# Seven products in place of four corners in one more unit, and two levels in one more product

## The chip, the cores and the metric

The kernel runs on one core of a Trainium2 chip. The metric is the device time of one execution, in microseconds, taken as the median of several runs. A core has five engines with a queue each: TensorE (PE in the profile, its weight loads PEld), VectorE (DVE), ScalarE (ACT), GpSimd (POOL) and SyncE (SP). Transfers run on 16 DMA engines; SP and POOL issue them here. The engines meet through semaphores, and every queue is worked off in its own order.

## The reference

Everything is float32 at the core; the inputs arrive as 64-bit floats. A block of linear attention with decay feeds a two-layer network:

```python
# q, k, v: (4, 8, 768, 64); lam: (8,), w_in: (512, 2048), w_out: (2048, 512)
# attention, by blocks of 64 tokens, with a running state per head:
out[block] = (q k^T * decay mask) v + (q * decay) state
state      = lam^64 * state + (k * decay)^T v
x = out as (3072 tokens, 512)
h = x @ w_in
y = (h - tanh(h)) @ w_out
```

Most of the work is in the last two matrix products, 3072 x 512 x 2048 each.

## The kernel before

**Tiling.** The tokens are worked in six groups (g = 0 to 5) of 512: 128 positions of each of the four sequences. For a group, attention gives x (transposed, in two halves `xt0`, `xt1` of two sequences each), the up stage gives the hidden values, and the down stage gives the group's 512 x 512 outputs. The hidden width, 2048, is cut in four units (u = 0 to 3) of 512.

**Fewer products.** A 2 x 2 block product takes eight block products when done plainly. Strassen's scheme in Winograd's form takes seven, P1 to P7, at the price of sums: of the left factor (`S1` to `S4`), of the right factor (`T1` to `T4`) and of the products. `FACT` (L523) names the two factors of each. `up(g, u, n)` does product n of unit u (4 matmuls of 256 columns, L554) with what follows it: ScalarE copies and tanh, VectorE adds and subtractions. For unit 3 of the first group the four corners are done plainly, by `up_plain` (8 matmuls of 256 columns for each corner, L966), and so for unit 0. The sums of a unit's input weights are made by `sums_in(u)` in `ws[u]` and, for S3, in place in `w1[u]`; for unit 3 this runs in the second group (L1150).

**Two levels.** A product can itself be done in seven (a second level). In the down stage `down_twice(g, n)` does so with 28 matmuls of 128 columns (L907), where `down(g, n)` takes 16 of 256 columns (L850). `twice(g, n)` says which is used. The second level needs the quarters and sums of the right factor, which are the same for all groups and are made once, in DRAM (`fine`): `load_quarters(t)` reads four quarters of the factor of product `MADE[t]` (5, 6, 4, 7, 3), `quarters_alone(t)` writes three of them out as they are, and `factors_twice(t)` makes four differences on VectorE and writes each out. `TURNS` (L1118) spreads this over steps of the second group's up stage for t = 0 and 1. The quarters of t = 0 lie in four tiles of the ring, those of t = 1 in output tiles, those of later t in a hidden tile (`gS`) that is free then.

**The ring.** The down stage's weights stream from DRAM through eight tiles (`wb`), in the order of `stream`; GpSimd issues each load, when a tile is free (L793, L796, L799).

**From the third group on** the up stage has a second level too: `inner_steps(g + 1, n)` runs between the products P3 of the group before (`in_turn`). It needs sums of the tokens (`inner_tokens`) and of the weights (`inner_weights`).

**Order.** The program is written in the order that the loops give; a planner at build time orders each engine's queue by that order and by when operands come, except where `keep_in_program_order` (`tied`) holds it. The first group's up stage is a list by hand, `turns` (L1077): for each entry a product or corner, then so many blocks of the output weights to be rounded (`weights`; three ScalarE and two VectorE operations each), then pieces of the second group's attention. A pair of sequences has five or six pieces: transposes, scores (L359), states (L434, L438, L440), the output's part from the state (`att_inter`, L479), its part within the block (`att_intra`, L498), and for the second pair the sums T of the tokens (`att_sums`). While `held` is set, between the fourth and the fifth piece, the matmuls in between keep the order of the program.

**First down stage.** The first group's down products run over eight steps (kt); step kt needs a pair of weight blocks, rounded, and their sums (`sums_out`). Every third pair uses `ws[3]` and `ws[0]` as its tiles. `sums_first` and `sums_late` make the sums of the hidden values, unit by unit.

**Banks.** Products accumulate in PSUM. Products of a unit use the tags `ya` or `yb` (even or odd u), `w` and `z`, one bank each; attention and others use four banks `att`. A bank is taken again when what is in it has been read.

The functions that the diff touches, and what calls them:

Of the kernel before, what the change touches and what calls it, by code (L numbers as in the profile page):

```python
# [24 lines left out]
def kernel(  # L25
# [225 lines left out]
    def pair_tiles(kt):  # L251

        if kt % 3 == 2:
            return tuple(ws[u].rearrange("p x k c -> p (x k) c")[:, 0:4] for u in (3, 0))
        wt = wst.tile([128, 8, 256], F32, name="wt", tag="w")
        return wt[:, 0:4], wt[:, 4:8]

    def sums_in(u):
        a11, a12, a21, a22 = (w1[u][:, 2 * c:2 * c + 2, r] for r, c in ((0, 0), (0, 1), (1, 0), (1, 1)))
        s1, s2, s4 = (ws[u][:, x] for x in range(3))  # L260
        for dst, x, y, op in ((s1, a21, a22, AL.add), (s2, s1, a11, AL.subtract), (a21, a11, a21, AL.subtract),
                              (s4, a12, s2, AL.subtract)):
            tc.keep_in_program_order(nc.vector.tensor_tensor(dst, x, y, op=op))
# [461 lines left out]
    def twice(g, n):  # L725
        return n in TWICE and not (g == NG - 1 and n == 3) and not (g == 1 and n == 4) and not (
            g <= GI and n in (7, 3))
# [32 lines left out]
    def load_quarters(t):  # L760

        for i in range(2):
            for j in range(2):
                if t == 0:
                    x = late["pool"].tile([128, NU, 128], F32, name="wq", tag="wb", bufs=RING)
                elif t > 1:
                    x = hidden(GI + (t > 2), "S1")[:, 2 * i + j].rearrange("p m (v c) -> p (m v) c", v=2)
                else:
                    x = opool.tile([128, NU, 128], F32, name="oq", tag="o")
                tied(t > 1, nc.gpsimd.dma_start(out=x, in_=quarter_source(t, i, j)))  # L770
                quarters[t, i, j] = x
# [124 lines left out]
    def down_twice(g, n, zw):  # L896
# [30 lines left out]
        elif n == 7:  # L927
            nc.vector.tensor_tensor(res[g, 4], res[g, 4], o, op=AL.add)
            store(g, 21, res[g, 4], g < NG - 1)
            nc.vector.tensor_tensor(o, o, res[g, 5], op=AL.add)  # L930
            store(g, 22, o, g < NG - 1)
        elif n == 3:
            nc.vector.tensor_tensor(o, o, res[g, 5], op=AL.add)
            store(g, 12, o)
# [20 lines left out]
    def up_plain(u, cs):  # L955

        hm = {}
        for c in cs:
            a, t = divmod(c - 11, 10)
            tag = ("yb", "w")[a ^ t] if u == NU - 1 else ("ya", "yb", "z", "w")[2 * t + a]  # L960
# [105 lines left out]
    for u, n in ((1, 2), (1, 6), (1, 5), (1, 7), (2, 1), (1, 4), (1, 3)):  # L1066
        up(0, u, n)
        weights(ready["done"] + 1 + (n == 2))
        if n == 5:
# [7 lines left out]
    turns = [(2, 5, 0, ()), (2, 2, 0, ()), (2, 6, 0, p0[0:1]), (3, 11, 0, p0[1:3]), (2, 7, 1, ()),  # L1077
             (3, 21, 0, p0[3:4]), (2, 4, 1, p0[4:]), (3, 12, 1, p1[0:1]), (2, 3, 1, p1[1:3]), (3, 22, 1, ())]
    for u, x, n, more in turns:
        if u == 2:  # L1080
            up(0, u, x)
        else:
            every(up_plain(u, (x,)))
        ahead = (u, x) == (2, 4)
        if ahead:
            run(more)
        weights(ready["done"] + n, True)
        if not ahead:
            run(more)
        if (u, x) == (2, 2):  # L1090
            held["yes"] = False
            sums_first(0)
    sums_out(0)
    weights(NU * KI + 4, True)
    for kt in range(KH):
# [10 lines left out]
        if kt == 3:  # L1106
            sums_first(NU - 1)
# [10 lines left out]
    TURNS = {t + x: n for n, t in ((0, 7), (1, 14)) for x in range(4)}  # L1118
    making = {}

    def make_factors(step):
        t = TURNS.get(step)
        if t is not None:
            if t not in making:
                making[t] = factors_twice(t)
            next(making[t])

# [6 lines left out]
    for g in range(1, NG):  # L1134
        last = g == NG - 1
        (p0, p1), step = ahead, 0
        for u in range(NU):
# [3 lines left out]
            if g < GI:  # L1141
                for n in (2, 6, 5, 7, 1, 4, 3):
# [6 lines left out]
                    if u == 0 and n == 5:  # L1149
                        sums_in(3)  # L1150
# [55 lines left out]
        if g < GI:  # L1206
            load_quarters(2)
# [9 lines left out]
        if g == GI:  # L1217
            load_quarters(3)
# [7 lines left out]
        if g in (1, GI):  # L1226
            quarters_alone(1 + g)
# [8 lines left out]
        for kind, x in in_turn(g):  # L1236
# [16 lines left out]
            if g < GI and (kind, x) == (4, 5):  # L1253
                every(factors_twice(2))
            if g == GI and (kind, x) == (1, 4):
# [43 lines left out]
```

## Time and profile before

| | |
|---|---|
| median of 3 runs | 645.86 us (643.43 to 646.31) |
| profiled execution | 642.59 us, span 640.8 us |
| TensorE (PE) busy | 632.3 us, 99%, 6424 instructions |
| VectorE (DVE) busy | 480.7 us, 75%, 956 instructions |
| ScalarE (ACT) busy | 270.9 us, 42% |
| GpSimd (POOL) busy | 221.6 us, 35% |
| read and written in DRAM | 216 GB/s over the span |
| granted TensorE clock | 1.00 throughout |

The span is from the first to the last instruction; the execution's own time has 1.8 us around it. Busy times add up what an engine has under way, so a matmul that overlaps the next one shows longer than what it adds. The chain is found by going back from the last instruction to what released it, step by step, so a line's share of it is time in which that line set the pace.

### The profile page before, as it was taken

Reading aid. Unit: us, or ns where it says so; the run is one execution under the profiler, and the core shown is the slowest. Engines: PE = TensorE matmul, PEld = TensorE weight load, DVE = VectorE, ACT = ScalarE, POOL = GpSimd, SP = SyncE. Lnnn points to the kernel's source line nnn. Section 1 sums busy time; section 2 is a strip of 40 time slices with the busy share of each in tenths; the row PEclk is TensorE's granted clock in tenths of the full one; section 3 lists DMA queues with packets and bytes.
Section 4 is the critical chain, followed back from the end, with each engine's and each line's share of the span. In section 5 each row is a group of like instructions: output and inputs, shape, how many; then the busy total and the mean of one; then the engine's idle time right before and its main releaser. Section 6 shows DMA issues by size and latency. Waiting matters only on the chain.

```text
span 640.8 us, 16604 instructions
## 1 busy us (share of the span) xinstructions
PE 632.3 (99%) x6424; PEld 580.8 (91%) x6424; DVE 480.7 (75%) x956; ACT 270.9 (42%) x626; POOL 221.6 (35%) x388
## 2 busy tenths in 40 slices
PE   8999999999999999999999999999999999999998
PEld 6788888888888999998999998999998899998997
DVE  4779697757888877579966589987658987467953
ACT  3898678403522422335431336243246332334310
POOL 0000135436623465311545730445321254421251
PEclk9999999999999999999999999999999999999999
DMA  9989899749956899876899994898873477732384
GB/s 211 230 230 246 224 280 303 268 120 287 306 134 171 244 298 316 234 159 132 246 272 279 268 318 111 212 278 266 226 194 77 136 240 239 247 107 76 100 300 144
DMA packets 166046, 139.80 MB, mean 218 GB/s; under 512 B 136720, under 2 KB 137872, under 8 KB 165968
## 3 DMA queue, kind: packets, MB, share of 16 engines
q0 software_dynamic: 31648, 104.62, 50.4%
q1 hardware_dynamic: 134176, 34.12, 26.2%
q8 instruction: 51, 0.84, 0.5%
q14 instruction: 27, 0.22, 0.1%
q10 hardware_dynamic: 144, 0.00, 0.0%
HBM read 111.94 MB, written 26.74 MB: 216 GB/s over the span
## 4 chain that ended last, share of the span: by engine, by line
PE 79%; issue 10%; POOL 4%; DMA 3%; DVE 2%; SPq 1%; ACT 1%; POOLq 0%
PE plain L850 12%; PE y L698 8%; PE y L907 8%; PE acc L995 7%; PE y L554 7%; PE zw L907 6%; PE z L698 4%; PE y L620 3%; PE zs L620 3%; PE z L554 3%; PE h L966 3%; POOL wb L796 2%; PE w L698 2%; PE w L554 2%; PE op L498 2%
## 5 line engine op out<-in xcount | busy, mean ns | idle before, releaser
L796 POOL DMA_DIRECT2D wb<-fine x133 | 71.6, 539 | 156.8 <-PE plain L850 107.9
L850 PE MATMUL plain<-wb,g 128*128 128x256 f32 x416 | 96.0, 381 | 0.0
L850 PEld LDWEIGHTS plain<-wb,g 128*128 128x128 f32 x416 | 77.5, 190 | 10.4
L911 ACT ACTIVATE q<-y 128x128 f32<-128x128 f32 x76 | 21.1, 277 | 85.2 <-PE y L907 84.1
L799 POOL DMA_DIRECT2D wb<-factors x64 | 34.5, 539 | 62.4 <-PE z L698 40.4
L907 PE MATMUL y<-wb,g 128*128 128x128 f32 x336 | 44.8, 278 | 0.0
L793 POOL DMA_DIRECT2D wb<-fine_in x60 | 32.5, 543 | 27.8 <-PE z L698 10.8
L601 ACT ACTIVATE th<-g 128x512 f32<-128x512 f32 x48 | 29.5, 627 | 29.4 <-DVE g L626 29.3
L907 PEld LDWEIGHTS y<-wb,g 128*128 128x128 f32 x336 | 40.7, 192 | 0.7
L689 ACT ACTIVATE g<-y 128x512 f32<-128x512 f32 x24 | 14.3, 597 | 63.1 <-PE y L698 63.1
L218 POOL DMA_DIRECT2D raw<-in_moe_w_out_dram x12 | 7.1, 592 | 87.8 <-ACT r L290 84.1
L401 ACT ACTIVATE k_nat<-k_nat,mask 128x64 f32<-128x64 f32 (+1 forms) x128 | 35.0, 336 | 0.6 <-DMA k_nat<-in_k_dram 0.6
L995 PE MATMUL acc<-wt,g 128*128 128x256 f32 x144 | 32.7, 380 | 0.0
L602 DVE TENSOR_TENSOR g<-g,th 128x512 f32<-128x512 f32 x48 | 32.0, 683 | 0.4
L698 PE MATMUL z<-tt,wb 128*128 128x128 f32 x256 | 31.9, 275 | 0.0
L966 PE MATMUL h<-xt,w 128*128 128x256 f32 x128 | 29.9, 383 | 1.2 <-DVE w L293 1.2
L995 PEld LDWEIGHTS acc<-wt,g 128*128 128x128 f32 x144 | 27.0, 190 | 4.1 <-DVE g L1003 0.4
L620 PE MATMUL y<-xt,w 128*128 128x256 f32 x128 | 30.3, 379 | 0.0
L620 PE MATMUL zs<-xt,ws 128*128 128x256 f32 x128 | 30.2, 379 | 0.0
L698 PEld LDWEIGHTS z<-tt,wb 128*128 128x128 f32 x256 | 30.2, 192 | 0.0
L907 PE MATMUL zw<-wb,g 128*128 128x128 f32 x224 | 30.1, 277 | 0.0
L966 PEld LDWEIGHTS h<-xt,w 128*128 128x128 f32 x128 | 23.6, 190 | 4.6 <-ACT xt L459 0.8
(237 smaller groups left out, 1541.6 us busy)
## 6 DMA issues: line engine op xcount, KB each, us to landing
wb<-fine POOLq DMA_DIRECT2D x133, 256.0 KB, 4.1
wb<-factors POOLq DMA_DIRECT2D x64, 256.0 KB, 4.4
wb<-fine_in POOLq DMA_DIRECT2D x60, 256.0 KB, 4.6
v_nat<-in_v_dram SPq DMA_DIRECT2D x24, 256.0 KB, 5.0
raw<-in_moe_w_out_dram POOLq DMA_DIRECT2D x12, 512.0 KB, 5.6
fine<-gS POOLq DMA_DIRECT2D x21, 256.0 KB, 6.0
k_nat<-in_k_dram SPq DMA_DIRECT2D x20, 256.0 KB, 5.3
raw<-in_moe_w_in_dram SPq DMA_DIRECT2D x8, 512.0 KB, 5.1
```

Of the source, the lines that this page charges most:

```text
L401: tc.keep_in_program_order(nc.scalar.activation(k_h, k_h, AF.Copy, scale=mask[0:rows, h % 2, h // 2, HALF - 1:HALF]))
L554: tied(held["yes"], nc.tensor.matmul(out=t[:, m, :], lhsT=wt[:, kt, ts(m, 128)], rhs=x[:, kt, :], start=first and m == 0 and kt == 0, stop ...
L602: nc.vector.tensor_tensor(dst(c), src, th, op=AL.subtract)
L620: nc.tensor.matmul(out=t[:, m, :], lhsT=wt[:, kt, ts(m, 128)], rhs=x[:, kt, :], start=False, stop=kt == 1, skip_group_check=True)
L698: nc.tensor.matmul(out=dst[:, ts(u, 128)], lhsT=a, rhs=b, start=(x in (1, 5) or x == 2 and not filled) and u == 0, stop=True, skip_group_c ...
L793: nc.gpsimd.dma_start(out=t.rearrange("p m c -> p (m c)"), in_=fine_in[INNER.index(n_[1]), (5, 6, 3).index(x_)].rearrange("p u c -> p (u c)"))
L796: nc.gpsimd.dma_start(out=t.rearrange("p m c -> p (m c)"), in_=fine[TWICE.index(n_), SUB.index(x_)].rearrange("p u c -> p (u c)"))
L799: nc.gpsimd.dma_start(out=t, in_=factors[XAT[FACT[n_][1]]][:, 2 * x_:2 * x_ + 2, :])
L850: tied(held["yes"], nc.tensor.matmul(out=t[:, m, :], lhsT=a[:, u, kt, ts(m, 128)], rhs=wb[:, kt, :], start=first and u == 0 and m == 0 and ...
L907: tied(held["yes"], nc.tensor.matmul(out=dst, lhsT=a[:, u, :], rhs=wb[:, ts(u, 128)], start=x in (1, 2) and u == 0, stop=u == NU - 1, skip ...
L966: tied(u == 0 or held["yes"], nc.tensor.matmul(out=hm[c][:, m, :], lhsT=w1[u][:, i, a, ts(m, 128)], rhs=xt[0, t][:, i, :], start=m == 0 an ...
L995: tied(held["yes"], nc.tensor.matmul(out=acc[n][:, r, :], lhsT=a[:, ts(r, 128)], rhs=b, start=kt == 0 and r == 0, stop=kt == KH - 1, skip_ ...
```

## The change

Three things, and what follows from them:

1. The first group's unit 3 is done by seven products (`up(0, 3, n)`), not by four plain corners. The list `turns` is written anew, with the products of unit 2 and unit 3 alternating. The sums of unit 3's input weights are made in two halves among them. As `ws[3]` is then used for an output pair, the second group rebuilds it from what is left (`sums_more`, three operations). `sums_first(0)` moves behind P5 of unit 3, and `sums_first(3)` goes, since P3 of a unit makes these sums itself. The two halves of each third pair change places (`pair_tiles`).
2. The factor of P4 (t = 2) gets its second level in the second group's up stage: loads at step 11, into four ring tiles, the three copies at step 17, the four differences at steps 18 to 21.
3. The place that this had at the end of the second group is taken by the factor of P7 (t = 3), which was made in the third group before. So P7 of the third group (g = 2) can run in two levels, and `twice` says so; the stores after it are issued at once, as P3 of that group is plain.

```diff
     def pair_tiles(kt):
         if kt % 3 == 2:
-            return tuple(ws[u].rearrange("p x k c -> p (x k) c")[:, 0:4] for u in (3, 0))
+            return tuple(ws[u].rearrange("p x k c -> p (x k) c")[:, 0:4] for u in (0, 3))
...
-    def sums_in(u):
+    def sums_in(u, which=range(4)):
...
-        for dst, x, y, op in ((s1, a21, a22, AL.add), (s2, s1, a11, AL.subtract), (a21, a11, a21, AL.subtract),
-                              (s4, a12, s2, AL.subtract)):
+        steps = ((s1, a21, a22, AL.add), (s2, s1, a11, AL.subtract), (a21, a11, a21, AL.subtract),
+                 (s4, a12, s2, AL.subtract))
+        for dst, x, y, op in (steps[n] for n in which):
+            tc.keep_in_program_order(nc.vector.tensor_tensor(dst, x, y, op=op))
+
+    def sums_more(u):
+        a11, a12, a22, s3 = (w1[u][:, 2 * c:2 * c + 2, r] for r, c in ((0, 0), (0, 1), (1, 1), (1, 0)))
+        s1, s2, s4 = (ws[u][:, x] for x in range(3))
+        for dst, x, y, op in ((s2, a22, s3, AL.subtract), (s1, s2, a11, AL.add), (s4, a12, s2, AL.subtract)):
             tc.keep_in_program_order(nc.vector.tensor_tensor(dst, x, y, op=op))
...
     def twice(g, n):
-        return n in TWICE and not (g == NG - 1 and n == 3) and not (g == 1 and n == 4) and not (
-            g <= GI and n in (7, 3))
+        return n in TWICE and not (g == NG - 1 and n == 3) and not (g < GI and n in (4, 7)) and not (
+            g <= GI and n == 3)
...
-                if t == 0:
+                if t in (0, 2):
                     x = late["pool"].tile([128, NU, 128], F32, name="wq", tag="wb", bufs=RING)
                 elif t > 1:
-                    x = hidden(GI + (t > 2), "S1")[:, 2 * i + j].rearrange("p m (v c) -> p (m v) c", v=2)
+                    x = hidden(GI + (t > 3), "S1")[:, 2 * i + j].rearrange("p m (v c) -> p (m v) c", v=2)
...
-            store(g, 21, res[g, 4], g < NG - 1)
+            store(g, 21, res[g, 4], twice(g, 3))
             nc.vector.tensor_tensor(o, o, res[g, 5], op=AL.add)
-            store(g, 22, o, g < NG - 1)
+            store(g, 22, o, twice(g, 3))
...
-    turns = [(2, 5, 0, ()), (2, 2, 0, ()), (2, 6, 0, p0[0:1]), (3, 11, 0, p0[1:3]), (2, 7, 1, ()),
-             (3, 21, 0, p0[3:4]), (2, 4, 1, p0[4:]), (3, 12, 1, p1[0:1]), (2, 3, 1, p1[1:3]), (3, 22, 1, ())]
+    turns = [(2, 5, 0, ()), (2, 2, 0, ()), (2, 6, 0, p0[0:1]), (3, 1, 0, ()), (2, 7, 0, p0[1:3]), (3, 2, 1, ()),
+             (2, 4, 1, p0[3:4]), (3, 6, 1, p0[4:]), (2, 3, 0, p1[0:1]), (3, 5, 1, ()), (3, 7, 0, p1[1:3]), (3, 4, 1, ()),
+             (3, 3, 0, ())]
     for u, x, n, more in turns:
-        if u == 2:
-            up(0, u, x)
-        else:
-            every(up_plain(u, (x,)))
-        ahead = (u, x) == (2, 4)
-        if ahead:
-            run(more)
+        up(0, u, x)
+        if (u, x) == (2, 6):
+            sums_in(NU - 1, (0, 1))
+        run(more)
         weights(ready["done"] + n, True)
-        if not ahead:
-            run(more)
         if (u, x) == (2, 2):
             held["yes"] = False
+        if (u, x) == (2, 7):
+            sums_in(NU - 1, (2, 3))
+        if (u, x) == (3, 5):
             sums_first(0)
...
-        if kt == 3:
-            sums_first(NU - 1)
...
-    TURNS = {t + x: n for n, t in ((0, 7), (1, 14)) for x in range(4)}
+    TURNS = {t + x: n for n, t in ((0, 7), (1, 14), (2, 18)) for x in range(4)}
...
+        if step == 11:
+            load_quarters(2)
+        if step == 17:
+            quarters_alone(2)
...
                     if u == 0 and n == 5:
-                        sums_in(3)
+                        sums_more(NU - 1)
...
         if g < GI:
-            load_quarters(2)
+            load_quarters(3)
...
-        if g == GI:
-            load_quarters(3)
...
-        if g in (1, GI):
-            quarters_alone(1 + g)
+        if g < GI:
+            quarters_alone(3)
...
             if g < GI and (kind, x) == (4, 5):
-                every(factors_twice(2))
-            if g == GI and (kind, x) == (1, 4):
                 every(factors_twice(3))
```

## The prediction

> **What bounds the kernel now.** I read the page's busy shares first, then the chain that ended last, then busy times in stretches of the first group, then single pieces of the chain for the price of a matmul.
>
> ```profile
> PE 632.3 (99%) x6424; PEld 580.8 (91%) x6424; DVE 480.7 (75%) x956; ACT 270.9 (42%) x626; POOL 221.6 (35%) x388
> PE 79%; issue 10%; POOL 4%; DMA 3%; DVE 2%; SPq 1%; ACT 1%; POOLq 0%
> ```
>
> TensorE (PE) is busy 99% of the 640.8 us span and carries 79% of the chain. Most of its 8 us of idle time lies in the first 32 us, which the change does not touch. So a matmul that goes is time that goes, unless TensorE then waits for something else. Prices, from the chain in order of time:
>
> ```profile
> 66.80 3.45 PE h L966 x16
> 182.68 1.73 PE y L554 x8
> 333.55 7.10 PE plain L850 x32
> 359.23 1.79 PE y L698 x16
> 436.85 0.89 PE y L907 x8
> ```
>
> One matmul in the code is two TensorE instructions in the trace: a product of a unit (L554) issues 4 matmuls and shows 8. With 256 columns, 8 instructions take 1.73 us, 216 ns each; with 128 columns, 16 take 1.79 us, 112 ns each. Halving the columns does not quite halve the price.
>
> Where the change adds VectorE work, these rows matter (stretch; its length; busy us of TensorE, its weight loads, VectorE, ScalarE, GpSimd with counts; clock; DMA):
>
> ```profile
> 57.60:63.20 5.60, 5.60 (x61) 4.81 (x63) 5.58 (x10) 3.34 (x7) 0.00 (x0) 1.00 1.16 305
> 63.20:77.50 14.30, 14.30 (x291) 12.35 (x283) 8.06 (x16) 8.80 (x20) 1.22 (x2) 1.00 0.99 249
> 77.50:93.50 16.00, 15.45 (x312) 13.06 (x311) 15.91 (x34) 10.76 (x22) 6.59 (x10) 1.00 0.84 235
> 160.00:184.40 24.40, 24.40 (x115) 21.48 (x114) 20.28 (x54) 11.45 (x27) 11.44 (x18) 1.00 0.76 233
> ```
>
> The first three are the end of the first group's up stage with the second group's attention between. VectorE (third pair of numbers) is full, then has 6.2 us free, then is full again; only in the full stretch does TensorE idle, 0.55 us. The last row is the second group's up stage, where VectorE has 4.1 us free.
>
> **The change part by part.**
>
> *Fourth unit of the first group.* Four plain corners are 4 x 8 matmuls, 64 instructions; seven products are 7 x 4, 56 instructions. 8 x 216 ns = 1.73 us less on TensorE, on the path.
>
> What it adds on VectorE: four sums of weights (the same four run later today),
>
> ```profile
> 145.07 0.68 DVE L263 TENSOR_TENSOR ws<-w 128x512 f32<-128x512 f32 x1
> 145.79 0.69 DVE L263 TENSOR_TENSOR ws<-ws,w 128x512 f32<-128x512 f32 x1
> 146.40 0.68 DVE L263 TENSOR_TENSOR w<-w 128x512 f32<-128x512 f32 x1
> 147.00 0.68 DVE L263 TENSOR_TENSOR ws<-w,ws 128x512 f32<-128x512 f32 x1
> ```
>
> whose starts are 0.60 us apart when nothing waits, so 2.4 us; and eight operations after the products (two adds, four subtractions after the tanh, two sums for the down stage) where the plain unit has four in this stage: another 2.4 us. In all 4.8 us. The two sums of unit 0 (1.2 us) go from 59.5 us to behind P5 of unit 3, near 77 us. Free before the stage ends are 6.3 us, less the 1.73 us by which it is shorter: 4.6. So VectorE would come out full, and what counts is where. Three rows bear on it:
>
> ```profile
> 87.69 0.64 DVE state L438
> 88.84 1.13 DVE state L440 x4
> 90.11 1.04 PE op L479 x54
> ```
>
> The states of the second token pair (L438, L440) are what TensorE waits for today, 0.3 us, before the state part of the attention output (L479); those matmuls have their order held, so what stands behind them stays there. From the state matmuls to L479 lie the time of two products and two sums of the down stage (3.45 + 1.73 us), as today. New ahead of L440: P7's add and subtraction and the two sums of unit 0, 2.4 us. Gone from ahead of it: the four operations behind unit 2's P3, 2.4 us, at 83 to 87 us today; P3 now comes before the second pair's transposes, so they fall into the free stretch, and so do two of the four sums; the other two replace unit 0's sums at 59.5. That is even to within an operation. The bounds: a gain of 0.55 us (today's idle goes) and a loss of 6.0 us (4.8 new and 1.2 moved, all exposed). I take a loss of 0.6, one operation's pitch, as the nearest row is a wait of 0.3. Other waits on VectorE here: P5 of unit 3 starts on the bank that unit 2's P3 leaves (one add, then the transposes lie between), P3 writes the bank that P7's add reads, 3.7 us after P7 with the scores, the states and P4 between, and the down stage's fifth sum starts on P3's bank, with two sums (8 instructions, 1.73 us) and L479 (1.1 us) between. Each wait is covered while VectorE is under 2 to 4 us late, and is in the 6.0.
>
> ScalarE gets three copies of 0.6 us, 1.8 us against 10.7 free in the two later stretches. The second pair's transposes come about 3.4 us earlier; their last K load was issued by 65.4 us and lands in 5.3 (page, DMA issues), near 70.7, against a start near 74: covered by about 3 us. Nothing else on SP's queue moves. The five weight blocks rounded among the turns stay five, at nearly the same times. The two halves of every third weight pair change places, so the half written first is that of unit 0, which nobody reads then: no cost.
>
> In the second group three sums instead of four rebuild the fourth unit's weights (0.6 us less), and the two sums of unit 3 at the fourth step of the first down stage go: VectorE has room at both.
>
> *Third factor in the second group's up stage.* Four loads, three copies out, four subtractions with four writes (256 KB each) now run between steps 11 and 21, 157 to 176 us. VectorE: 4 x 0.6 = 2.4 us into 4.1 free; the products there use alternate banks, and today's later stretch with VectorE busy for all of its 14 us (386 to 400) shows no TensorE wait. GpSimd's queue: 11 issues, about 4 x 0.75 + 7 x 0.55 = 6.9 us into 13 free, with the fine weights of the inner level and the ring's first pieces queued behind the ones that wait for loads (6.2 us landing in the middle). The loads use four of the ring's eight tiles. In the ring today:
>
> ```profile
> 155.12 2.13 POOL L799 DMA_DIRECT2D wb<-factors  x4
> 165.32 1.11 POOL L799 DMA_DIRECT2D wb<-factors  x2 [0.87 <-DMA fine<-wq]
> ```
>
> and the pieces are first read at 184.4 (first four) and 196.8 us (next four). If the next four wait until the last write of the new quarters has landed (176 + 1 + 6, by the first quarters' rows), they are issued by 184 and there by 189: covered by 8 us, so I take nothing. Without the cover the price is what they are late by; the upper bound is one landing and one issue chain, 4.4 + 2.1 = 6.5 us.
>
> *P7 of the third group in two levels.* Plain: 16 matmuls, 32 instructions x 216 ns = 6.91 us. Two levels: 28 matmuls, 56 instructions x 112 ns = 6.27 us. Saved 0.64 us; the fourth group's P7, already so, has its pieces at 0.89 per 8, the same price. The Trainium skill, "TensorE: Matmul & The Clock Gate", section "Back-to-back issue gap", gives 134 and 262 cycles for 128 and 256 columns, a ratio of 1.955 where these rows have 1.93. By that ratio the two levels would take 56 x 110.5 ns = 6.19 us and save 0.72; the row decides, and the difference is nothing in the sum.
>
> It adds on VectorE three sums, one correction and two net operations behind the product, 6 x 0.6 = 3.6 us, and four 0.28 us copies on ScalarE; in 330 to 341 us VectorE has 3 of 10 us free, and the fourth group does the same with TensorE full throughout. Three more pieces (256 KB) go through the ring; the eleven GpSimd issues that made this factor (the loads from 331.8 us, its four subtractions, 2.4 us, to 355.6) leave the third group at just this place. The second group's late quarters are now those of P7, in the place that P4's had. No cost taken; bounds a gain of 0.3 (a wait like L440's) and a loss of one operation chain behind P6, 1.5 us, if its tile is late for P7's copy.
>
> **Sum.** 642.59 (the profiled execution, span 640.8) - 1.73 - 0.64 + 0.6 = 640.8 us, 0.28% less. The runs' median is 645.86, 3.27 above the profiled one, and they spread over 643.43 to 646.31; carried to the median: 644.1. I give 644.0.
>
> **Rivals.**
> *All of it and the idle too.* Today's 0.55 us of idle goes and nothing comes: 642.59 - 2.37 - 0.55 = 639.7, 643.0 on the median, 0.46% less. For it: VectorE is relieved of unit 2's tail just where TensorE waits. Against: it is full on balance.
> *VectorE late (slower).* Its surplus all stands before the states in the held order: +6.0 instead of +0.6 gives 646.2, 649.5 on the median, 0.56% more. It decides against the change once L440 is over 2.4 us late, and passes 0.5% from 5.6. For it: 15.91 of 16 busy and a wait on L440 already there. Against: 6.2 us free just before. The same page of the Trainium skill lists VectorE's queue as strict first-in first-out, which is what would turn one late operand into a late state; the rows above show only the order, so it changes no number here.
> *Ring late.* The quarters hold the ring's tiles too long and the plain P2 of the second group waits 3 us (half the bound): 640.2 + 0.6 + 3 = 643.8, 647.1 on the median. Against: 8 us of cover.
> *The products save nothing.* That the instruction counts don't fall is excluded by the loops.
>
> **How the numbers follow.** The forecast has 0.57, all and the idle 0.20, VectorE late 0.12 (anything over 2.4 us), the ring 0.11. A half per cent (3.2 us) is about what a measurement tells from no change. With the runs' spread of 0.2% either way, half of the second case and an eighth of the first pass -0.5%: 0.17, with rounding 0.18; some two thirds of the third and a quarter of the ring pass +0.5%: 0.11; the rest 0.71. The range reaches from 640.8 (forecast, at the profiled run's level) to 648.0 (VectorE about 4.5 us late).
>
> **What would show it.** TensorE's instruction count falls by 8 and rises by 24, to 6440; its busy time falls by about 2.4 us. Right: the first down stage's matmuls (L995 today) start 1 to 2 us earlier than 87.6 us; P7 of the third group shows 56 narrow instructions at 0.89 per 8. Wrong: a TensorE wait on the state operation (L440), on the add behind P7 or P3 of unit 3, or on a ring piece near 197 us, longer than 1 us. A low granted clock would make it wrong too; it is 1.00 in every row above.

## The result and the profile after

The changed kernel takes 649.82 us (median of 8 runs, 646.78 to 651.44), the kernel before 644.72 us beside it (8 runs, 642.58 to 647.98): a ratio of 1.0077, 95% interval 1.0052 to 1.0103. It is slower by 0.8% where 0.28% faster was predicted. Four of the eight runs ended at 650.9 to 651.4 with a mean granted clock of 0.994 to 0.997, the other four at 646.8 to 648.7 with 1.000; the profiled execution (651.44 us, span 649.6) is one of the first four, the slowest of the eight, and that clock turns out to be part of the story.

The page's busy times and its chain:

```profile
PE 633.2 (97%) x6440; PEld 582.2 (90%) x6440; DVE 487.0 (75%) x967; ACT 273.5 (42%) x633; POOL 222.8 (34%) x391
PE 80%; DVE 7%; ACT 5%; DMA 4%; SPq 2%; issue 2%; ACTq 0%
```

TensorE (PE) has the 6440 instructions that were predicted, but its idle time has doubled, from 8 us to 16, and VectorE and ScalarE now stand in the chain with 7% and 5%. The view of TensorE's waits (us in total, times, the longest) says for whom it idles; the first three rows and the two smaller ones are new:

```profile
PE kv L441 <- issue: 3.0, 2, 2.6
PE y L627 <- ACT y L617: 2.8, 2, 1.7
PE acc L1002 <- DVE g L1009: 1.5, 1, 1.5
...
PE zw L914 <- DVE g L920: 0.6, 1, 0.6
...
PE acc L1002 <- DVE g L588: 0.3, 1, 0.3
```

Where the time goes is read best from the starts of the same TensorE work in both traces (us from the span's start):

| TensorE starts | before | after | difference |
|---|---|---|---|
| first matmul of the first down stage | 87.59 | 85.46 | -2.13 |
| its last matmul ends | 139.35 | 138.60 | -0.75 |
| state part of the attention output, third group's attention, first pair | 203.83 | 203.08 | -0.75 |
| the same, second pair | 228.18 | 227.97 | -0.22 |
| fourth group's attention, first pair | 305.75 | 309.45 | +3.70 |
| second pair | 329.37 | 339.69 | +10.32 |
| fifth group's, first pair (P7 lies between) | 406.94 | 416.67 | +9.73 |
| end of the span | 640.79 | 649.63 | +8.85 |

So the first group gains what was forecast and gives two thirds of it back; then 3.9 us are lost between 228 and 305 us and 6.6 us between 305 and 340 us, neither in a place where the change has a TensorE instruction; and P7 gives its 0.6 us. I take the three losses in turn.

**VectorE in the first down stage.** The stretches that the prediction used, in the trace of after (TensorE, weight loads, VectorE, ScalarE, GpSimd; clock; DMA):

```profile
63.20:77.50 14.30, 14.30 (x293) 12.53 (x283) 12.92 (x26) 11.99 (x27) 4.08 (x7) 1.00 1.08 277
77.50:93.50 16.00, 14.15 (x301) 11.85 (x300) 16.00 (x34) 10.59 (x24) 3.45 (x6) 1.00 0.91 269
160.00:184.40 24.40, 24.40 (x115) 21.48 (x114) 21.41 (x53) 11.58 (x28) 15.31 (x25) 1.00 0.97 280
```

VectorE went from 8.06 to 12.92 us busy in the free stretch, as planned, and is busy for all 16.00 us of the next, where TensorE now idles 1.85 us. The timeline of TensorE there (start, duration, the idle before and who ended it):

```profile
87.28 1.16 PE L486 MATMUL op<-qd,state 64*64 64x64 f32 x64
88.77 1.13 PE L1002 MATMUL acc<-wt,gS 128*128 128x256 f32 x4 [0.33 <-DVE g L588]
...
92.52 1.78 PE L1002 MATMUL acc<-wt,g 128*128 128x256 f32 x7 [1.53 <-DVE g L1009]
```

The state matmuls (L486, L479 before) wait for nothing any more. The waits have moved on. L588 is the add behind unit 3's P3, and the fifth sum of the down stage starts on the bank that it reads. L1009 is the late sums of the hidden values, which stand in VectorE's order behind unit 3's last operations and the sums of the next weight pair.

**The loads on SP's queue.** The third row of the stretches shows DMA at 0.97 and 280 GB/s where it was 0.76 and 233: the moved quarters are now made in it. SP issues the attention's loads in order, and the issues after that stretch come later and later. SP's timeline of before, then of after:

```profile
173.78 8.22 SPq L153 DMA_DIRECT2D k_blk<-in_k_dram  x16
211.74 8.46 SPq L153 DMA_DIRECT2D k_blk<-in_k_dram  x16
277.84 0.39 SPq L140 DMA_DIRECT2D k_nat<-in_k_dram  x1
```

```profile
173.54 11.65 SPq L153 DMA_DIRECT2D k_blk<-in_k_dram  x16
218.56 11.39 SPq L153 DMA_DIRECT2D k_blk<-in_k_dram  x16
284.07 0.38 SPq L140 DMA_DIRECT2D k_nat<-in_k_dram  x1
```

The batch of K blocks takes 11.65 us instead of 8.22, the next shown starts 6.8 us later, and the fourth group's first natural K is issued at 284.07 instead of 277.84, though TensorE is by then a fifth of a microsecond early. Behind that load stands ScalarE. The timeline of before (first line), then of after:

```profile
282.48 1.06 ACT L401 ACTIVATE k_nat<-k_nat,mask 128x64 f32<-128x64 f32 x4 [0.58 <-DMA k_nat<-in_k_dram]
```

```profile
287.35 1.06 ACT L408 ACTIVATE k_nat<-k_nat,mask 128x64 f32<-128x64 f32 x4 [5.67 <-DMA k_nat<-in_k_dram]
288.32 0.58 ACT L617 ACTIVATE y<-g 128x512 f32<-128x512 f32 x1
288.95 1.35 PE L627 MATMUL y<-xt,w 128*128 128x256 f32 x5 [1.11 <-ACT y L617]
```

ScalarE stands 5.67 us at the masking of k_nat (0.58 us before), the copy that frees TensorE's bank (L617) is queued behind it, and TensorE waits 1.11 us for it and 1.73 us more for the next such copy at 296 us: 2.84 of the 3.9 us.

**A stop for nothing that the profile names, and the clock behind it.** The chain in order of time, from 326 us:

```profile
326.58 0.56 PE kv L441 x35
327.14 2.59 issue
329.73 1.12 PE kv L441 x29
330.86 2.00 PE y L914 x8
332.86 1.71 PE zw L914 x8
334.57 1.62 PE y L914 x8
336.19 0.89 PE zw L914 x8
```

Sixty-four matmuls of one kind, in the middle of which the profile names nothing to wait for, run as 35, a pause of 2.59 us, and 29. Then eight narrow instructions take 2.00, 1.71 and 1.62 us instead of 0.89. The same time in stretches, with the granted clock as the third number from the end:

```profile
329.70:336.50 6.80, 6.77 (x58) 6.65 (x58) 2.77 (x7) 0.55 (x2) 1.09 (x3) 0.54 0.41 77
336.50:339.70 3.20, 3.20 (x32) 3.08 (x30) 1.29 (x5) 0.28 (x2) 2.13 (x4) 1.00 0.79 227
```

After the pause the clock is 0.54 for 6.8 us. That costs (1.12 - 0.68) + (2.00 + 1.71 + 1.62 - 3 x 0.89) = 3.1 us (0.68 us is what these 29 matmuls take after such a pause at full clock, below). With 2.59 for the pause and 0.55 for a wait on VectorE at 316.6 us (L920) this makes 6.2 of the 6.6 us.

Counting every instruction on TensorE's queue through the trace from 0 (matmuls, weight loads and the 230-odd for semaphores), the pause lies at number 6337 = 24 x 256 + 193, and a packet of 16,384 bytes on the queue that the page lists as "q8 instruction" starts at 327.03 us, 0.11 us before TensorE stops. The small pause in the same view (0.41 us at 220.8 us) lies at number 4033 = 15 x 256 + 193. Seven products are 8 matmuls and 8 weight loads fewer than four corners, so from the end of the first group's up stage on every instruction has a number 16 lower than before, up to P7 of the third group. The theory to be tested was therefore: three separate losses (VectorE's order, SP's order, the place of the instructions in the stream), none of them in TensorE's work. The rivals: that the quarters and P7 are the whole loss; that late loads bring about the pause too; that the pause is chance.

### The profile page after: what moved, and what is told of

It reads as the page before. It is cut to its first block, busy times and chain, and to the rows that moved or that the text cites. A ratio compares the mean times of both kernels' runs of the same rounds, so it can differ in the third digit from the quotient of the medians.

```text
span 649.6 us, 16665 instructions
## 1 busy us (share of the span) xinstructions
PE 633.2 (97%) x6440; PEld 582.2 (90%) x6440; DVE 487.0 (75%) x967; ACT 273.5 (42%) x633; POOL 222.8 (34%) x391
## 4 chain that ended last, share of the span: by engine, by line
PE 80%; DVE 7%; ACT 5%; DMA 4%; SPq 2%; issue 2%; ACTq 0%
PE y L914 11%; PE plain L857 11%; PE y L705 9%; PE zw L914 8%; PE acc L1002 7%; PE y L561 6%; PE z L705 5%; PE y L627 3%; PE zs L627 3%; PE z L561 3%; PE w L705 2%; PE w L561 2%; DMA q_blk<-in_q_dram 2%; SPq L153 1%; PE op L486 1%
## 5 line engine op out<-in xcount | busy, mean ns | idle before, releaser
L803 POOL DMA_DIRECT2D wb<-fine x140 | 75.4, 539 | 171.3 <-PE plain L857 110.6
L857 PE MATMUL plain<-wb,g 128*128 128x256 f32 x384 | 88.7, 381 | 0.0
L857 PEld LDWEIGHTS plain<-wb,g 128*128 128x128 f32 x384 | 71.5, 190 | 9.5
L806 POOL DMA_DIRECT2D wb<-factors x60 | 32.3, 540 | 57.6 <-PE z L705 38.9
L914 PE MATMUL y<-wb,g 128*128 128x128 f32 x360 | 49.0, 281 | 0.0
L914 PEld LDWEIGHTS y<-wb,g 128*128 128x128 f32 x360 | 44.4, 195 | 0.8
L914 PE MATMUL zw<-wb,g 128*128 128x128 f32 x240 | 33.3, 283 | 0.6 <-DVE g L920 0.6
L914 PEld LDWEIGHTS zw<-wb,g 128*128 128x128 f32 x240 | 30.0, 196 | 1.1 <-DVE g L920 0.7
L627 PEld LDWEIGHTS y<-xt,w 128*128 128x128 f32 x128 | 23.9, 190 | 7.1 <-ACT y L617 3.6
```

What stands on the lines that cost most here:

```text
L627: nc.tensor.matmul(out=t[:, m, :], lhsT=wt[:, kt, ts(m, 128)], rhs=x[:, kt, :], start=False, stop=kt == 1, skip_group_check=True)
L803: nc.gpsimd.dma_start(out=t.rearrange("p m c -> p (m c)"), in_=fine[TWICE.index(n_), SUB.index(x_)].rearrange("p u c -> p (u c)"))
L806: nc.gpsimd.dma_start(out=t, in_=factors[XAT[FACT[n_][1]]][:, 2 * x_:2 * x_ + 2, :])
L857: tied(held["yes"], nc.tensor.matmul(out=t[:, m, :], lhsT=a[:, u, kt, ts(m, 128)], rhs=wb[:, kt, :], start=first and u == 0 and m == 0 and ...
L914: tied(held["yes"], nc.tensor.matmul(out=dst, lhsT=a[:, u, :], rhs=wb[:, ts(u, 128)], start=x in (1, 2) and u == 0, stop=u == NU - 1, skip ...
```

## Experiments

Times are medians. Ratios are to the kernel before on the same chip, with 95% intervals; they weigh all the runs and are not the quotients of the medians. One execution of each kernel was profiled.

**One part alone.** e1_unit keeps only the seven products, e2_p7 only the moved quarters with P7 in two levels.

```diff
 e1_unit, against after
-            g <= GI and n == 3)
+            g <= GI and n in (7, 3))
-        if step == 11:
-            load_quarters(2)
-        if step == 17:
-            quarters_alone(2)
 ...
 e2_p7, against after
-    turns = [(2, 5, 0, ()), (2, 2, 0, ()), (2, 6, 0, p0[0:1]), (3, 1, 0, ()), ...
+    turns = [(2, 5, 0, ()), (2, 2, 0, ()), (2, 6, 0, p0[0:1]), (3, 11, 0, p0[1:3]), ...
 ...
```

> Only the fourth unit in seven products; quarters and P7 as before. Theory (separate losses; the largest comes from the moved quarters): the first down stage starts 2.1 us earlier than before, the wait for the late sums (1.5 us) takes most of it back, no wait of ScalarE for a K load near 285 us; in all 0.5 to 1 us faster than before (ratio 0.9985 to 0.9995). Rival (VectorE's surplus in the first group is the cause and carries on): 3 us or more slower than before.

> Only the quarters moved and P7 of the third group in two levels; the fourth unit plain as before. Theory: the loads on SP fall 6 us behind by 280 us, ScalarE waits 5 to 6 us for the K load, the third group's first state output is 4 us late, P7 gives back 0.6: 3 us or more slower than before (ratio 1.005 or more), without any wait in the first down stage. Rival (the fourth unit is the cause): 0.6 us faster than before.

Measured: e1_unit 645.77 against 643.23 us, 1.0037 [1.0008, 1.0066]; e2_p7 646.25 against 643.23, 1.0048 [1.0032, 1.0065]. Each part alone loses, and the two add up to 0.85% against the 0.77% of both. In e1_unit's profile TensorE is 0.64 us ahead until 305 us and 2.95 behind at the second pair of the fourth group's attention: the pause at the same number, 6337, here without the low clock.

```profile
322.20 0.74 PE L441 MATMUL kv<-v_nat,k_nat 64*64 64x64 f32 x35
325.26 0.68 PE L441 MATMUL kv<-v_nat,k_nat 64*64 64x64 f32 x29 [2.32 <-issue]
```

e2_p7 has no pause there (its instructions keep the numbers of before until P7); it loses from 228 to 305 us, +1.05 to +3.58 us, with k_nat issued at 282.53, ScalarE standing 4.1 us and TensorE's wait on the copy 1.7 us. (It is 0.58 us late from the start: its first score matmuls take 1.93 us instead of 1.16, and the trace has the granted clock at 0.50 from 7.75 to 11.16 us.) In e1_unit k_nat is issued at 279.84 us; ScalarE stands 1.88 us for it and TensorE loses nothing there. So the two losses come apart by part: the place in the stream goes with the seven products, the late loads with the quarters.

**The loads' order.** e3_early_k is the changed kernel with the natural K and V loads of the fourth group's first two sequences issued ahead of the third sequence's blocks; only SP's order differs.

```diff
+            early_k = (0, 1) if g == GB + 1 else ()
             for b in range(B - 1):
+                if b == 2:
+                    for b_ in early_k:
+                        load_natural(g, b_, nat)
                 load_blocks(g, b, "qk")
+            first = first + early_k
```

> The changed kernel with one edit: the fourth group's K and V loads of its first two sequences stand one batch of small loads earlier in SP's queue; every other queue is the same, instruction for instruction. Theory: ScalarE's wait for the K load (5.7 us) and TensorE's two waits behind it (2.8 us) go; 3 to 4 us faster than the changed kernel, so within 0.2% of before. Rival (the loss there is from the ring or from VectorE): the waits stay and the time is the changed kernel's.

Measured: 642.9 against 643.23 us, 0.998 [0.9957, 1.0003]. The loss between 228 and 305 us is gone: TensorE is 0.55 us ahead at the first and 0.56 ahead at the second. ScalarE starts the masking at 281.25 us with no wait in front of it. K issued late was the cause of that loss; the four other profiles with the early K lose nothing there either. The pause before number 6337 is still there, 1.67 us of the 2.3 us that TensorE loses between 305 and 331 us.

**Other places in the stream.** e4_shift puts 32 more small matmuls (64 matmul instructions and 64 weight loads in the trace) into the warm-up ahead of everything.

```diff
     for _ in range(8):
         nc.tensor.matmul(out=idle[:, 0:128], lhsT=ident, rhs=ident, start=True, stop=True)
+    for _ in range(32):
+        nc.tensor.matmul(out=idle[0:64, 0:64], lhsT=ident[0:64, 0:64], rhs=ident[0:64, 0:64], start=True, stop=True)
```

> The changed kernel with 32 small matmuls more (64 weight loads, 64 matmul instructions) ahead of everything, while TensorE waits for the first load; every other instruction in the same order. Theory (the 2.59 us stop within the state matmuls is TensorE's instructions arriving late): the stop moves to another place or goes, and with it the drop of the granted clock; up to 5 us off the executions that had it. Rival (the stop waits for data): the stop stays at the same matmul, with the same length.

Measured: 653.59 against 643.23 us, 1.0156 [1.0094, 1.0219]. As a measure of time it failed: the longer front itself delays the first down stage by 3.8 us (89.24 against 85.46). In the trace the new matmuls run from 5.07 to 9.61 us, and the first transposes start at 9.55 instead of 5.03 us. For the places it is plain: nothing stops at 327 us, and the pauses have moved to numbers 1217 (0.80 us at 67.5 us) and 8898 (1.67 us at 431.6 us), which leave 193 and 194 when divided by 256.

```profile
430.60 0.99 PE L443 MATMUL kv<-v_nat,k_nat 64*64 64x64 f32 x55
433.27 0.38 PE L443 MATMUL kv<-v_nat,k_nat 64*64 64x64 f32 x9 [1.67 <-issue]
```

**The old places back.** One warm-up matmul in the code is two matmuls and two weight loads in the trace, so four more of them give every later instruction the number that it had before the change (up to P7 where that runs in two levels). e5_page is e3_early_k with 12 warm-up matmuls instead of 8, e11_unit_page is e1_unit with 12, e12_after_page the changed kernel with 12.

```diff
-    for _ in range(8):
+    for _ in range(12):
         nc.tensor.matmul(out=idle[:, 0:128], lhsT=ident, rhs=ident, start=True, stop=True)
```

> The changed kernel with the early K and V loads, and twelve matmuls on the identity ahead of everything in place of eight (16 more TensorE instructions, in the idle time before the first load). From the first group's unit 3 to the third group's P7 each TensorE instruction then has the same place modulo 256 as before the change. Theory (TensorE stops at the place 193 modulo 256 of its instruction stream, where a new 16 KB piece of it has to arrive): the stop in the state matmuls near 322 us (1.7 to 2.6 us) goes; 1 to 2 us faster than the kernel with early loads alone. Rival (the stop has to do with the data of that block): it stays.

> Only the fourth unit in seven products, as in the run that was 0.37% slower than before, with 16 TensorE instructions more in front, so that all later ones have their places of before again. Theory (that run's loss is the stop at a place in the instruction stream, not the products): the stop near 322 us goes, ratio to before 0.997 to 0.9995. Rival (VectorE's load in the first group costs it): 1.003 or more again.

> The changed kernel with nothing but 12 warm-up matmuls in place of 8: every later TensorE instruction keeps the number it has in the kernel before; the order of the loads on SP's queue stays as the change has it. If the loss has two separate causes, the late loads and the place in the instruction stream: the second token pair's stage of the third group (near 305 us) still starts 3 to 4 us later than before, with ScalarE waiting over 3 us for k_nat; no stop with "issue" over 1 us near 320 to 330 us and the clock at 1.00 there; the median is about 645 to 647, a ratio of 1.002 to 1.006. If the late loads themselves bring the stop about: a stop of 1.5 us or more stays near 327 us, and the ratio is 1.006 or more. If the places alone made the loss: no wait of ScalarE for k_nat over 2 us, and a ratio of 0.996 to 0.998.

| | 8 warm-up matmuls | 12 (numbers of before) |
|---|---|---|
| seven products alone | 1.0037 [1.0008, 1.0066] | 0.9984 [0.9973, 0.9995] |
| the whole change | 1.0077 [1.0052, 1.0103] | 1.0026 [0.9999, 1.0054] |
| the whole change, K early | 0.998 [0.9957, 1.0003] | 0.9971 [0.9953, 0.9989] |

Sixteen instructions that compute nothing make the first two rows faster by half a per cent. The kernel before with 12 was not run, but a better warm start is not what the profiles show: with 12 the first down stage starts at 85.43, 85.95 and 86.25 us, with 8 at 85.64, 85.46 and 85.53 us (rows in order). In all three profiles on the right the 64 matmuls run through; e11_unit_page's:

```profile
320.61 1.16 PE L366 MATMUL sp<-qt,kt 64*64 64x64 f32 x64
321.59 1.11 PE L441 MATMUL kv<-v_nat,k_nat 64*64 64x64 f32 x64
322.63 1.16 PE L914 MATMUL y<-wb,g 128*128 128x128 f32 x8
```

e12_after_page speaks against the rival that late loads bring about the pause. Its waits:

```profile
PE y L627 <- ACT y L617: 1.7, 1, 1.7
PE acc L1002 <- DVE g L1009: 1.5, 1, 1.5
...
PE kv L441 <- issue: 0.4, 2, 0.2
```

K is as late as ever (issued at 282.08, ScalarE stands 4.05 us, TensorE loses 2.6 us between 228 and 305), and no pause is longer than 0.24 us. The two losses are separate, as far as one profile of each shows: e12_after_page and e2_p7 have the late K without the pause at 6337, e1_unit has the pause without the loss from a late K. In the third row the shift buys only 0.1%, within both intervals, and e6_late_sums below, which also has the change's own numbers, shows no pause at 6337.

The traces give a size for it. The instruction at 6337 is one of those 64 matmuls in both cases; only the 256 before it differ. With the numbers of before they take 5.34 us (seven profiles: the kernel before, e2_p7, e5_page, e7_both, e9_both_again, e11_unit_page, e12_after_page; no pause in any). With the numbers of the change the block begins 16 instructions further on in the program, so that it holds eight 128-column matmuls fewer and eight small ones more, and without the pause it takes 4.56 to 4.84 us (after, e1_unit, e3_early_k, e6_late_sums and e8_before_page with the two runs like it). So the next block has 0.5 to 0.8 us less to arrive in.

That is the smaller part. Each trace has 51 packets of 16,384 bytes on q8, as many as TensorE's queue has whole blocks of 256. Taken in order, packet n starts at least 2.2 us before instruction 256 n + 193 in all fifteen profiles, and each of the fifteen pauses over 0.3 us ends 2.2 to 3.0 us after its packet's start. So TensorE stops where it has used up one block before the packet of the next is 2.2 to 3.0 us old, be it that the block is short or that the packet starts late. At 6337 it is the packet:

| profile | packet starts, us after instruction 6081 | pause |
|---|---|---|
| after | 4.72 | 2.59 |
| e1_unit | 4.55 | 2.32 |
| e3_early_k | 4.06 | 1.67 |
| e13_before_page_third | 2.90 | 0.44 |
| ten others (e4_shift has other work there) | -1.06 to 0.80 | none |

With the packet of after, a block of 5.34 us would still have left a pause of about 2 us (an estimate: 4.72 + 2.70 - 5.34, the pause having ended 2.70 us after the packet's start). The packet is late in four of the seven profiles with the change's numbers and in none of the seven with those of before. Late packets go with busy DMA engines: in the 3 us after the instruction that opens a block the mean DMA share is 0.61 where the packet has started by then, and 1.00 where it starts 3 us later or more. But before 6337 that share is 0.97 or more in all fourteen, so traffic alone does not tell late from prompt. What makes a packet late in one place and one execution and not in the next is open, and so is how the numbering brings it about.

**VectorE's order.** e6_late_sums is e3_early_k with the first late sums issued before the state part of the second pair's attention output, and so before the sums of the next weight pair; e7_both and e9_both_again have the early K, the early sums and 12 warm-up matmuls.

```diff
         if kt == 0:
+            sums_late(0)
             run(p1[3:4])
 ...
-        sums_late(kt)
+        if kt > 0:
+            sums_late(kt)
```

> The changed kernel with the early K and V loads, and the first down step's late sums (sums_late of step 0) ahead of the next step's weight sums on VectorE; all other queues the same. Theory (VectorE is late by its order there): TensorE's wait of 1.53 us on them goes, the first down stage ends 1.2 to 1.5 us earlier, and so does the kernel, 0.2% faster than with early loads alone. Rival (VectorE is full, so the wait only moves): another wait of about 1.5 us comes in the next two steps of the down stage.

> The changed kernel with all three: early K and V loads, late sums ahead, 16 more TensorE instructions in front. Theory: the saving of 2.4 us that was predicted stands at last, and the stops are gone: 2 to 4 us faster than before (ratio 0.994 to 0.997). Rival: within 0.2% of before.

> The kernel with early K and V loads, late sums ahead and 16 TensorE instructions in front once more, with more rounds, for a narrower interval: 0.996 to 0.998 of before if its gain is one, 0.999 to 1.001 if it is not.

Measured: e6_late_sums 641.89 against 642.82 us, 0.9981 [0.9963, 0.9999]; e7_both 641.07 against 642.82, 0.997 [0.993, 1.0009]; e9_both_again 641.19 against 643.03, 0.9964 [0.995, 0.9978]. Against e3_early_k (0.998) and e5_page (0.9971), which lack it, the sums' new order is worth nothing that can be measured. TensorE's timeline of e9_both_again says why:

```profile
88.80 1.13 PE L1007 MATMUL acc<-wt,gS 128*128 128x256 f32 x4 [0.30 <-DVE g L593]
89.86 1.16 PE L510 MATMUL op<-ss,v_nat 64*64 64x64 f32 x64
90.95 5.45 PE L1007 MATMUL acc<-wt,g 128*128 128x256 f32 x24
...
99.97 2.07 PE L1007 MATMUL acc<-wt,g 128*128 128x256 f32 x8 [0.98 <-DVE g L1014]
```

The wait of 1.53 us at 91 us is gone and one of 0.98 us stands at 99 us, at the late sums of the next step (L1014 again), as the rival had it: VectorE, being full, passes its lateness on. From there on this version is 0.8 us ahead of the kernel before in every row of the table above, -1.39 after P7, and ends 2.18 us earlier. It has the lowest ratio; the intervals of e5_page, e6_late_sums and e11_unit_page lie below 1 too.

**The kernel before with fewer instructions.** If 16 numbers are all, the kernel before with 4 warm-up matmuls instead of 8 should show the loss too; e8_before_page, e10_before_page_again and e13_before_page_third are that one kernel.

```diff
-    for _ in range(8):
+    for _ in range(4):
```

> The kernel before the change with four matmuls on the identity in front in place of eight: 16 TensorE instructions fewer, which puts all later ones at the places that the fourth unit in seven products puts them; nothing else is changed. Theory (places in the instruction stream): a stop of 1.5 to 2.6 us comes in the state matmuls near 322 us, and the time rises by 2 us or more over before, with no work added. Rival: the time is that of before.

> The kernel before with four identity matmuls fewer in front once more: its first profile was of one of its quickest executions and had no stop. Theory (places in the instruction stream): a profile of a usual execution has stops of 1 us or more in blocks of 64 x 64 matmuls, at the place 193 modulo 256, and no other wait that before has not. Rival (the shorter warm-up): the time is lost in the first 60 us.

> The kernel before with 4 warm-up matmuls in place of 8, profiled once more, for an execution that isn't its quickest. If the places alone cost it its 0.4 to 0.5%: a profiled execution above 645 us shows a stop with "issue" of 1 to 3 us in the small square matmuls of the attention, at an instruction number of 193 to 194 modulo 256, most likely the 6337th near 322 us. If it is the shorter warm-up: such an execution shows the milestones late from the first 60 us on, by 2 us or more, and no such stop.

Measured: 646.39 against 642.82 us, 1.004 [1.0015, 1.0065]; 645.92 against 643.03, 1.005 [1.003, 1.0069]; and two executions of 649.2 and 652.41 against 644.26, 1.0102 [1.0065, 1.014]. It is slower, but not for the reason tested. The first two profiles (643.1 and 643.2 us, the quickest executions of theirs) are 0.9 and 0.8 us late at the first down stage and 0.6 at the end. The third, 652.41 us, is already 3.17 us late at the first down stage, with no pause so far. At its start the scores' 16 matmuls take 2.08 us in two places (e10_before_page_again: in one, at 7.99 us):

```profile
7.96 2.08 PE L374 MATMUL sp<-qt,kt 64*128 64x128 f32 x16 [0.69 <-ACT kt L339]
12.62 2.08 PE L374 MATMUL sp<-qt,kt 64*128 64x128 f32 x16 [0.69 <-ACT kt L339]
```

In the kernel before, with 8 warm-up matmuls, both take 1.16 us. The clock records of the three traces with 4 begin, at full clock, only at 11.17, 11.36 and 17.2 us, those of before at 6.61 us; that the clock is the reason for the 2.08 us fits with e2_p7's slow start but is not shown. So a shorter warm-up costs time at the start, which spoils the test: pauses at 4033, 6337 and 9153 are there, but only 0.39, 0.44 and 1.17 us long. That profile holds a second surprise. It has none of the moved quarters, and yet its k_nat is issued at 287.63 us, ScalarE stands 5.34 us for it, and TensorE loses 3.6 us between 228 and 305 us:

```profile
PE y L620 <- ACT y L610: 2.5, 2, 1.7
...
PE y L907 <- issue: 1.2, 1, 1.2
```

So the moved quarters are one way to make SP late and not the only one. In the profiles in which the quarters run early and K is in its old place, k_nat is issued at 282.1 to 287.6 us (four profiles); without them at 276.5 to 280.9 (five) and 287.6 (this one; it and e4_shift are about 3 us behind the kernel before at the end of the first group already). That it is the quarters' traffic that slows SP is argued from the rows above; no run took the traffic away and left the rest.

## Why the prediction was wrong

**Fourth unit, "8 x 216 ns = 1.73 us less on TensorE, on the path".** Right, and a little more: the first down stage starts 2.13 us earlier (between 1 and 2 was forecast), which is 1.73, the wait of 0.3 for the keys' copy (L359 before) that also went, and 0.1 more.

**"That is even to within an operation. ... I take a loss of 0.6."** The size was off and the place wrong. I looked for VectorE's lateness at the states (L440), where the old wait of 0.3 us was; the states come in time, and what is late is what stands last in VectorE's order, the operations for the next products of the down stage (L588 0.33, L1009 1.53 us). The first of the two is on the prediction's list of covered waits, the fifth sum on P3's bank; the second is not on it. Of 2.13 us, 0.75 is left at the stage's end: a term of 1.4 instead of 0.6. The rival "VectorE late" named the right engine, with up to 6.0; it took this much and no more.

**"P7 of the third group in two levels ... Saved 0.64 us".** Right: the difference changes by -0.59 us across it in after, e3_early_k and e9_both_again, with 0.89 us per eight narrow instructions. No wait came on VectorE or the ring.

**"Third factor ... I take nothing."** The step that failed first. I priced the four loads and four writes by the queue that issues them, by VectorE and by the tiles of the ring, and covered the ring by 8 us: no ring piece was late. I did not price what they do to SP's loads. "Nothing else on SP's queue moves" was true of the order and false of the times: SP's batches of 16 K blocks go from 8.2 to 11.7 us, the lag adds up over 100 us, and it ends at a ScalarE instruction that stands in order in front of a copy for TensorE. ScalarE had no time in hand even before (it waits 0.58 us for that load); the row was there to be read. TensorE had a little: where ScalarE stands 1.88 us (e1_unit) it loses nothing between 228 and 305 us, where ScalarE stands 4.05 and 5.67 us (e12_after_page, after) it loses 2.6 and 3.9 us. The price: 1.0026 against 0.9984 with the numbers of before, 0.42% or 2.7 us, with P7's gain of 0.6 inside it.

**"A low granted clock would make it wrong too; it is 1.00 in every row above."** It came, behind a pause for which the sum had no term and the rivals no place. Removing instructions was taken as moving time only. It also renumbers TensorE's instructions, and with the new numbers came a pause of 0.4 to 2.6 us in four of seven profiles: giving the old numbers back is worth 0.5% in two of the three rows of the table. The pause is 2.3 of the 3.3 us by which e1_unit's profile is longer than e11_unit_page's. The Trainium skill, "Runtime: NRT & Kernel Launch", section "Instruction fetch mechanics", says that an engine's instructions come in 16 KiB blocks of 256 and that crossing a block is mostly hidden. The period of 256 and the 16,384-byte packet agree with it; the pauses of 1.67, 2.32 and 2.59 us do not agree with hidden. They came where 256 instructions were used up in under 5 us, in the attention's small matmuls, behind a packet that started 4.1 to 4.7 us after the first instruction of the block before; why it did, no run shows.

With both repaired, the runs fit the sum: -0.28% was predicted, 0.9971 and 0.9964 were measured (e5_page, e9_both_again, the latter with VectorE's sums moved too). That e9_both_again's profiled span falls by 2.18 us where the sum had 1.77 is partly luck. It is 0.8 in the first group (1.13 was forecast), 0.6 for P7, and 0.8 in the last group, where the change does nothing; e8_before_page and e10_before_page_again gain 0.6 and 0.8 us there too, so this part belongs to the profiled execution of before.

Open: why the fetch is late in some executions only; what else than the quarters makes SP late (e13_before_page_third); and whether that lateness is also why runs of the kernel before spread over 642 to 648 us, as no late execution of it was profiled. The version with K early is not free of such runs: e7_both has four at 640.4 to 641.2 us and two at 645.0 and 645.5, these two with a mean granted clock of 0.997.

## What to carry to other kernels

Ask of moved DMAs what they do to every in-order queue that is loading at the time, and follow each such load to the instruction that waits for it and to what is queued behind that one; a wait of half a microsecond in the trace of before says that the engine which waits has no time in hand, and the next engine little. A kernel with thousands of short matmuls has a cost that belongs to no instruction: when adding or removing a few changes the time by half a per cent elsewhere, look for "issue" in the middle of a group of like matmuls, count the instructions modulo 256, look when the instruction packet before that place started, and try a few idle instructions at the front. A full engine hands its lateness to whatever stands last in its order, so look there, not where the wait is today.

## What the hardware showed that was not expected

- TensorE can stop in the middle of 64 like matmuls for 0.3 to 2.6 us. Every stop of a matmul over 0.3 us put down to "issue" in the fifteen profiles (fifteen stops in ten of them, thirteen within the 64 x 64 matmuls) lies at an instruction number that leaves 193 or 194 when divided by 256, and ends 2.2 to 3.0 us after the start of its 16,384-byte packet on q8.
- One stop of 2.59 us was followed by 6.83 us at half clock (by the trace's clock records), stops of 2.32 and 1.67 us by none. The Trainium skill, "TensorE: Matmul & The Clock Gate", section "What's actually happening", asks for at least one idle window of about 3.4 us; here less was enough, while 6.83 us is twice that window.
- Four warm-up matmuls instead of eight left 16 score matmuls at 2.08 us instead of 1.16, once or twice, within the first 15 us, and in the worst profile the first down stage came 3.2 us late. Eight do not rule it out: in e2_p7 the same 16 took 1.93 us once, at a granted clock of 0.50.
